# Rewrite of a gated attention and linear-attention kernel: row-tiled scores, column-tiled P.V, exponentials shared between ScalarE and VectorE, instruction order from a list scheduler

## Chip, cores, metric

One core of one Trainium2 chip. Times are device microseconds (us) of one execution; most are medians of four runs. A profiled run also has a span (first to last instruction, about 1.9 us less than its time) and a mean granted TensorE clock, where 1.0 is full speed.

## The reference

Two attention blocks read the same x (2048 x 512, 32 heads of 16) and are mixed by a gate. Block A is softmax attention, block B linear attention. Shortened:

```python
g = sigmoid((x * gate_w).sum(-1, keepdims=True))
# A: per head, Dh = 16
p = softmax(einsum("bhqd,bhkd->bhqk", q, k) * Dh ** -0.5)
a = einsum("bhqk,bhkd->bhqd", p, v)  ... @ A_wo
# B: phi(t) = where(t > 0, t + 1, exp(t)) + 1e-6
b = phi(q) @ (phi(k)^T v) / (phi(q) @ sum(phi(k)))  ... @ B_wo
return g * a + (1 - g) * b
```

Block A costs 32 heads x 2048 x 2048 exponentials: 2048 blocks of 128 keys x 512 queries. That decides the time.

## The kernel before

The kernel works in 32 rounds of four heads and 512 queries, 64 blocks each. K is copied four times with all but one head's 16 rows set to zero, so that a score matmul can read all 128 rows of the array. Three blocks at a time land in three banks of PSUM (the memory that matmuls write to; the kernel lays it out as eight banks of 512 columns), ScalarE exponentiates all three in one instruction, and P.V takes P as the weights and V (with a column of ones for the denominator) as the moving operand. VectorE has the projections' copies, the K masks and block B.

```python
# scores: full array, K zero-padded to one head
f_mm(RINGB[b0 + k], KTpad[:, hs, j, 128 * kb:128 * (kb + 1)], QT[:, par, qc, :], start=True, stop=True)
# exponentials: three banks, 128x1536, in one instruction
nc.scalar.activation(PT[:, slot, 0:512 * n], ps[:, 512 * b0:512 * (b0 + n)], ACT.Exp, scale=SCALE)
# P.V: 12 small matmuls a group, 128 x 32 out
f_mm(acc[:, 128 * qbl + 32 * j:128 * qbl + 32 * (j + 1)],
     PT[:, slot, 512 * k + 128 * qbl:512 * k + 128 * (qbl + 1)], Vaug[:, hs, kb, j, :], start=first, stop=False, sg=True)
# ... (projections, block B, gate and output are cut)
```

The softmax here doesn't subtract the row's maximum and nothing guards it: scores larger than these inputs give would overflow.

## Time and profile before

| | before |
|---|---|
| time, median (range) | 972.5 us (972.0 to 973.2) |
| ScalarE busy | 945.0 us, 97% of the span |
| TensorE busy, mean granted clock | 832.4 us, 0.993 |
| VectorE busy | 305.9 us, 32% |

ScalarE is the bound: 934.2 us of exponentials with 10.6 us idle before them, most of that before the first one. TensorE waits for ScalarE, not the other way round.

One stretch of the steady part, from the view of windows. The columns are the busy us of TensorE, weight loads, VectorE, ScalarE and GpSimd, then the granted clock, DMA share and GB/s.

```profile
300.00:500.00 200.00, 173.42 (x2316) 104.56 (x2358) 65.64 (x139) 199.80 (x160) 0.00 (x0) 1.00 0.01 2
```

### The profile page before, as it was taken

How to read it: one execution, taken by the hardware profiler on the slowest of the kernel's cores; microseconds unless marked ns; L12 is line 12 of the kernel's file. 1: busy time of each engine (PE TensorE's matmuls, PEld its weight loads, DVE VectorE, ACT ScalarE, POOL GpSimd, SP SyncE). 2: the span in 40 equal slices, each digit the busy share in tenths (PEclk: the TensorE clock that was granted, in tenths of full speed). 3: DMA queues.
4: the chain of work that ended last, by engine and by line, in shares of the span. 5: the costliest groups of instructions: out<-in, count | busy, mean ns of one | idle time of the engine just before them, and what ended most of it. 6: DMA issues, size and time to landing. Idle time of an engine off the chain costs nothing.

```text
span 970.5 us, 25037 instructions
## 1 busy us (share of the span) xinstructions
PE 832.4 (86%) x11257; PEld 504.8 (52%) x11464; DVE 305.9 (32%) x591; ACT 945.0 (97%) x739; POOL 8.1 (1%) x42
## 2 busy tenths in 40 slices
PE   6988888898888988888888888888888898879886
PEld 3555555555555555555545555554555555545553
DVE  3311132032321223223654445344555431102112
ACT  3999999999999999999999999999999999999996
POOL 3000000000000000000000000000000000000000
PEclk8999999999999999999999999999999999999998
DMA  9000000000000000000000000000000000000001
GB/s 275 3 2 1 2 2 1 2 1 2 2 2 2 2 1 2 1 2 2 2 1 2 2 1 2 2 1 1 1 2 2 1 2 1 1 2 18 12 18 45
DMA packets 13067, 10.40 MB, mean 11 GB/s; under 512 B 6816, under 2 KB 11936, under 8 KB 12960
## 3 DMA queue, kind: packets, MB, share of 16 engines
q1 hardware_dynamic: 8768, 7.34, 2.5%
q10 hardware_dynamic: 4192, 1.44, 0.7%
q8 instruction: 90, 1.47, 0.6%
q14 instruction: 17, 0.14, 0.1%
HBM read 5.64 MB, written 2.10 MB: 8 GB/s over the span
## 4 chain that ended last, share of the span: by engine, by line
ACT 52%; PE 30%; issue 14%; DVE 2%; DMA 1%; ACTq 1%; DVEq 0%
ACT PT L730 51%; PE ps L307 30%; DVE den L613 1%; ACT epool L514 1%; DMA wA_5<-in_A_wqkv_dram 1%; DVE tpool L516 1%; ACTq L273 0%; DVE outt L677 0%; DVE den L607 0%; PE ps L310 0%; DMA out_dram<-outt 0%; DVE KTpad L425 0%; ACTq L992 0%; ACTq L985 0%; DVE KT L413 0%
## 5 line engine op out<-in xcount | busy, mean ns | idle before, releaser
L730 ACT ACTIVATE PT<-ps 128x1536 bf16<-128x1536 f32 (+1 forms) x704 | 934.2, 1465 | 10.6 <-PE ps L307 9.5
L307 PE MATMUL ps<-QT,KTpad 128*128 128x512 bf16 x1883 | 529.4, 381 | 116.6 <-ACT PT L730 108.4
L307 PEld LDWEIGHTS ps<-Vaug,PT 128*128 128x128 bf16 x8192 | 308.0, 96 | 166.7 <-ACT PT L730 0.8
L307 PE MATMUL ps<-Vaug,PT 128*128 128x32 bf16 x8192 | 313.8, 176 | 1.0 <-ACT PT L730 0.4
L307 PEld LDWEIGHTS ps<-QT,KTpad 128*128 128x128 bf16 x2048 | 152.4, 97 | 247.6 <-ACT PT L730 139.9
L756 DVE RECIPROCAL rden<-ps 128x16 f32<-128x16 f32 x32 | 8.2, 257 | 190.8 <-PE ps L307 190.8
L613 DVE RECIPROCAL den<-den 128x128 f32<-128x128 f32 x64 | 61.0, 953 | 2.2
L516 DVE COPY tpool<-ps 128x512 f32<-128x512 f32 x32 | 22.1, 691 | 91.0 <-ACT epool L514 91.0
L465 DVE CAST Vaug<-ps 128x256 bf16<-128x256 f32 x32 | 13.6, 424 | 78.9 <-PE ps L307 78.9
L425 DVE TENSOR_SCALAR KTpad<-KT,maskK 128x512 bf16<-128x512 bf16 x128 | 34.6, 346 | 0.1
L307 PE MATMUL ps<-wB,xT 128*128 128x512 bf16 x116 | 31.1, 377 | 3.1 <-DVE tpool L516 2.6
L564 DVE TENSOR_TENSOR kvacc<-ps,kvacc 128x258 f32<-128x258 f32 x32 | 13.7, 428 | 57.4 <-PE ps L307 57.4
L307 PE MATMUL ps<-xT,wA 128*128 128x512 bf16 x100 | 27.0, 377 | 0.5
L482 DVE CAST QT<-ps 128x512 bf16<-128x512 f32 x16 | 11.1, 691 | 42.4 <-PE ps L307 42.4
L413 DVE CAST KT<-ps 128x512 bf16<-128x512 f32 x16 | 11.1, 692 | 39.4 <-PE ps L307 39.4
L514 ACT ACTIVATE epool<-ps 128x512 f32<-128x512 f32 x32 | 21.8, 682 | 0.0
L677 DVE SCALAR_TENSOR_TENSOR outt<-ps,gom,bB 128x512 bf16<-128x512 f32 x16 | 11.8, 749 | 28.3 <-PE ps L307 26.8
L645 DVE TENSOR_SCALAR bB<-ps,gom 128x512 bf16<-128x512 f32 x16 | 12.0, 750 | 26.6 <-PE ps L307 26.6
L607 DVE TENSOR_SCALAR den<-ps 128x512 f32<-128x512 f32 x16 | 11.1, 691 | 29.6 <-PE ps L307 29.6
L307 PE MATMUL ps<-wA,xT 128*128 128x64 bf16 x448 | 18.7, 192 | 0.0
L307 PE MATMUL ps<-woA,OT 128*128 128x512 bf16 x58 | 16.6, 390 | 0.8 <-DVE OT L667 0.6
L667 DVE COPY OT<-ps 128x512 bf16<-128x512 bf16 (+2 forms) x20 | 7.1, 369 | 30.9 <-PE ps L310 30.9
(61 smaller groups left out, 246.1 us busy)
## 6 DMA issues: line engine op xcount, KB each, us to landing
out_dram<-outt SPq DMA_DIRECT2D x16, 128.0 KB, 1.7
wA<-in_A_wqkv_dram SPq DMA_DIRECT2D x1, 1536.0 KB, 7.0
wB<-in_B_wqkv_dram SPq DMA_DIRECT2D x1, 1536.0 KB, 10.3
xnat<-in_A_x_dram ACTq DMA_DIRECT2D x2, 512.0 KB, 5.3
woA<-in_A_wo_dram SPq DMA_DIRECT2D x1, 512.0 KB, 11.3
woB<-in_B_wo_dram SPq DMA_DIRECT2D x1, 512.0 KB, 12.2
wA_5<-in_A_wqkv_dram ACTq DMA_DIRECT2D x3, 128.0 KB, 6.9
xT<-in_A_x_dram SPq DMA_TRANSPOSE x8, 6.0
```

Of the source, the lines that this page charges most:

```text
L307: return lambda: nc.tensor.matmul(o, lhsT=l, rhs=r, start=start, stop=stop, skip_group_check=sg)
L413: op(DV, lambda par=par, t=t, sp_=sp_: nc.vector.tensor_copy(KT[:, par, 512 * t:512 * (t + 1)], sp_), reads=[rsp], writes=[r_KT[par][t]])
L425: op(DV, lambda hs=hs, j=j, t=t, par=par, half=half: nc.vector.tensor_scalar(KTpad[:, hs, j, 512 * t:512 * (t + 1)], KT[:, par, 512 * t:51 ...
L465: op(DV, lambda hs=hs, vb=vb, nb=nb, src=src: nc.vector.tensor_copy(Vaug[:, hs, vb:vb + nb, :, 0:16], src), reads=[rsp], writes=[r_Vaug[hs ...
L482: op(DV, lambda par=par, qc=qc, sp_=sp_: nc.vector.tensor_copy(QT[:, par, qc, :], sp_), reads=[rsp], writes=[r_QT[par][qc]])
L514: ev_e = op(AC, lambda e_s=e_s, sp_=sp_: nc.scalar.activation(epool[:, e_s, :], sp_, ACT.Exp), reads=[rsp], writes=[r_e[e_s]])
L516: op(DV, lambda e_s=e_s, sp_=sp_: nc.vector.tensor_copy(tpool[:, e_s, :], sp_), reads=[rsp], writes=[r_t[e_s]], extra=[ev_e])
L564: op(DV, lambda srcv=srcv, dstv=dstv: nc.vector.tensor_tensor(dstv, srcv, dstv, ALU.add), reads=[rsp, r_kvacc], writes=[r_kvacc])
L613: op(DV, lambda s=s, c4=c4: nc.vector.reciprocal(den[:, s, 128 * c4:128 * (c4 + 1)], den[:, s, 128 * c4:128 * (c4 + 1)]), reads=[r_den[s]] ...
L645: op(DV, lambda qc=qc, qbl=qbl, qb=qb, sp_=sp_: nc.vector.tensor_scalar(bB[:, qc, qbl, :], sp_, gom[:, 1, qb:qb + 1], None, op0=ALU.mult), ...
L677: op(DV, lambda s3=s3, qb=qb, qc=qc, qbl=qbl, sp_=sp_: nc.vector.scalar_tensor_tensor(out=outt[:, s3, :], in0=sp_, scalar=gom[:, 0, qb:qb ...
L730: op(AC, lambda slot=slot, b0=b0, n=n: nc.scalar.activation(PT[:, slot, 0:512 * n], ps[:, 512 * b0:512 * (b0 + n)], ACT.Exp, scale=SCALE), ...
```

## The change

The intent is to take exponentials off ScalarE. VectorE gets about a fifth of the key blocks and computes 2^t as the mean of four shifted piecewise-linear terms: the score plus a constant, written as int16, is the bit pattern of a bf16 near 2^t, and three more terms are that integer plus 26, 56 and 94. All four are multiplied with V as if they were four P blocks, so such a block costs four P.V waves (a wave is up to four tiled matmuls that run at the same time; in the trace one P.V wave starts 0.22 us after another at full clock) instead of one. To make room on TensorE, scores read only their 32 rows (four heads at once) and P.V makes V the weights, 17 columns in one of four column tiles, four heads at once. A list scheduler at build time picks the order and gives each key block to ScalarE or VectorE. Core of the diff, much cut:

```diff
-                fns.append(f_mm(RINGB[b0 + k], KTpad[:, hs, j, 128 * kb:128 * (kb + 1)], QT[:, par, qc, :],
-                                start=True, stop=True))
+            return mm(bank(b), KT[32 * j:32 * (j + 1), t8 % 2, 128 * kb:128 * (kb + 1)],
+                      Qz[32 * j:32 * (j + 1), qslot(r), par, :])
 ... (cut)
+            return C(DV, 400, 692, lambda: nc.vector.tensor_scalar(
+                Z[:, z, 512 * j:512 * (j + 1)], bank(5), ZB, 0.0, op0=ALU.add, op1=ALU.max),
 ... (cut)
+            return C(DV, 300, 690, lambda: nc.vector.tensor_scalar(Z[:, z, :], Z[:, z0, :], float(m), None, op0=ALU.add),
 ... (cut)
+            return C(AC, 500, 427 * n + 63, lambda: nc.scalar.activation(
+                P[:, slot, 0:512 * n], bank(b0, n), ACT.Exp, scale=ESC),
 ... (cut)
+            for j in range(4):
+                fns.append(mm(ps[32 * j:32 * j + 17, 3584:4096], Vc[:, t8 % 2, w["kb"], 2 * j + par, 0:17], w["aps"][j],
+                              start=first, stop=False, sg=True))
 ... (cut: the scheduler's choice of the next instruction)
+                if c.E is PE and c.mode and c.mode != st["mode"]:
+                    a = max(a, PE.free + 40.0)
```

PSUM is split into a set of three banks and one of two for ScalarE, one bank for VectorE's scores, one for everything else and one accumulator.

## The prediction

> **What bounds the kernel now.** ScalarE. The profile's busy table gives it 945.0 of 970.5 us (97%); the windows show it busy 199.3 to 199.8 us in each 200 us from 100 to 900. Nearly all is one group, the softmax exponentials: 704 activations, 934.2 us. From 16.6 to 961 us ScalarE works through 32 rounds of 20 three-bank and 2 two-bank exponentials and one 512-wide one; solved with one fixed cost per instruction beside 1280, 853 and 427 ns of streaming, that is 77 ns: 1.357, 0.930 and 0.504 us (estimates). TensorE is 86% busy but waits 109 us for ScalarE, VectorE is 32% busy, GpSimd 1%. Head 16.6 us, tail after the last exponential about 8.5 us.
>
> **What the change does** (counts from the instruction order).
> - ScalarE: exponentials fall from 640 three-bank + 64 two-bank (2048 score blocks) to 323 + 323 + one single (1616 blocks). 432 blocks, 21%, go to VectorE. ScalarE: 323 x (1.357 + 0.930) + 33 x 0.504 + about 4 = 760 us, 185 us less.
> - VectorE: 432 conversions out of PSUM at 0.691 us (the trace's duration for 128x512 fp32 from PSUM) = 299 us; 324 adds over 128x2048 int16. [...] I estimate 0.69 us each = 224 us; about 190 other operations, 130 us. Sum 650 us, up from 306.
> - TensorE: 8192 narrow P.V matmuls become 3344 in 836 column-tiled waves of four (1728 of them, 432 waves, for spline terms); the scores are row-tiled by four without the masked K copies. At 0.216 us for each concurrent wave (512 columns; estimate): scores about 800 x 0.216 = 173, P.V 181, rest 138: 490 us, plus about 1490 switches between tilings. [...] no trace here shows its cost yet. [...]
> - GpSimd: about 130 real operations, [...]
>
> **How much lies on the critical path.** ScalarE stays the bound, so its 185 us are nearly all worth time, but it will no longer be 99.9% fed: its two score buffers are three and two banks, [...] TensorE's fixed order also waits for VectorE. I allow 5 to 8% idle in ScalarE's steady stretch, 40 to 60 us. Head about 11 us (K and Q weights first, first block of x by small loads), tail about 9 us. 11 + 760 + 45 + 9 = 825 us. Range 790 to 870.
>
> Chances: faster by over 2% 0.95, within 2% 0.03, slower 0.02.
>
> **What would show it.** ScalarE 755 to 770 us busy, 90 to 95% of the span, idle before exponentials put down to score matmuls; VectorE 640 to 690 us, int16 adds 0.69 us undisturbed; score and P.V groups of four ending within about 0.25 us beyond one matmul's latency; first exponential at 10 to 13 us.
>
> **What would make it wrong.** Tiled matmuls that don't run concurrently (then TensorE alone needs over 1100 us); [...] tiling switches above 0.2 us, making TensorE the bound at 850 us or more; or a schedule matching the chip better than I allow, about 790 us.

The forecast's sum is whole: 11 + 760 + 45 + 9 = 825 us. In the trace of the kernel before, 128x512 matmuls start 0.216 us after one another (median), and activations that follow one another without a wait start 1.330 us apart over three banks and 0.477 us over one; over two it is 0.904 us in the changed kernel's trace, so about 0.427 us a bank.

## More of the kernel before

From the profile page of the kernel before: busy time of each engine, the busy tenths of ScalarE and the granted TensorE clock in 40 slices of the span, and the costliest group (busy us, mean ns of one, then idle time before them).

```profile
span 970.5 us, 25037 instructions
...
PE 832.4 (86%) x11257; PEld 504.8 (52%) x11464; DVE 305.9 (32%) x591; ACT 945.0 (97%) x739; POOL 8.1 (1%) x42
...
ACT  3999999999999999999999999999999999999996
...
PEclk8999999999999999999999999999999999999998
...
L730 ACT ACTIVATE PT<-ps 128x1536 bf16<-128x1536 f32 (+1 forms) x704 | 934.2, 1465 | 10.6 <-PE ps L307 9.5
L307 PE MATMUL ps<-QT,KTpad 128*128 128x512 bf16 x1883 | 529.4, 381 | 116.6 <-ACT PT L730 108.4
```

The clock row, which is easily passed over, is at 9 (90% or more) in all but the first and last slice.

## The result

| | before | after |
|---|---|---|
| time, median | 972.5 us | 880.1 us (872.9 to 888.3) |
| ratio to before, 95% interval | | 0.9025 (0.899 to 0.906) |
| ScalarE busy | 945.0 us | 770.9 us, 89% |
| TensorE busy | 832.4 us | 789.5 us, 91% |
| mean granted clock, profiled run | 0.993 | 0.855 |

A ratio here is always the mean time of one kernel's fast runs over that of the other's fast runs of the same rounds, so it isn't quite the ratio of the medians. One of the four runs (888.3 us, clock 0.834) counts as slow, being over 1.5% above the fastest, and is left out of the ratio. Clock and time go together within the four: 0.834 and 0.855 are the ends of one, 888.3 and 872.9 us of the other.

The change is clearly faster, but it misses the forecast of 825 us and its range of 790 to 870. The same page lines as before, of the changed kernel, with the chain of work that ended last by engine (the line that begins with PE 65%):

```profile
span 871.0 us, 15840 instructions
...
PE 789.5 (91%) x6283; PEld 210.7 (24%) x6345; DVE 625.0 (72%) x978; ACT 770.9 (89%) x686; POOL 145.4 (17%) x155
...
ACT  5999999877999988999798999978879779899984
...
PEclk7999999865999979999597999968759569699966
...
PE 65%; ACT 15%; DVE 11%; issue 9%; DMA 0%; POOL 0%; ACTq 0%; SPq 0%; POOLq 0%
...
L631 ACT ACTIVATE P<-ps 128x1536 bf16<-128x1536 f32 (+1 forms) x647 | 753.5, 1263 | 75.9 <-PE ps L323 73.0
L576 DVE TENSOR_SCALAR Z<-ps 128x512 int16<-128x512 f32 x432 | 295.6, 684 | 182.4 <-PE ps L323 180.4
L598 DVE TENSOR_SCALAR Z<-Z 128x2048 int16<-128x2048 int16 x324 | 228.0, 731 | 3.4
```

Put the ACT and PEclk rows under each other: ScalarE's dips lie where the clock is low. The busy work came out as planned (770.9 us on ScalarE, 625.0 on VectorE). What is new is 75.9 us of idle time before exponentials, 73.0 of it put down to TensorE, and TensorE's 65% of the chain that ended last.

The view of windows of the changed kernel, for a stretch at half clock and the next at full clock:

```profile
620.00:650.00 30.00, 28.95 (x169) 5.34 (x162) 17.20 (x26) 21.39 (x19) 4.03 (x4) 0.50 0.05 10
652.00:674.00 22.00, 18.67 (x186) 5.26 (x182) 18.98 (x32) 22.00 (x20) 1.24 (x3) 1.00 0.05 13
```

At half clock TensorE is busy 28.95 of 30 us and ScalarE only 21.39. At full clock ScalarE is busy all 22.00. Over the whole steady part I cut the trace at every change of the clock and summed such windows: ScalarE is busy 75.1% of 206 us at half clock and 96.9% of 577 us at full clock. The recorded clock is only ever 1.0 or 0.5 (44 stretches), in stretches that are multiples of 3.41 us (the last, cut off by the end, aside); a mean of 0.855 is 29% of the span, 253 us, at half speed.

What half clock does to one wave (here of 512 columns) is in the timeline of TensorE's matmuls (start us, us, then what). First a stretch at half clock:

```profile
632.23 1.03 PE L323 MATMUL ps<-Z,Vc 128*17 128x512 bf16 x8
633.20 0.60 PE L323 MATMUL ps<-Qz,KT 32*128 32x512 bf16 x2
633.74 0.61 PE L323 MATMUL ps<-P,Vc 128*17 128x512 bf16 x4
634.27 1.03 PE L323 MATMUL ps<-Qz,KT 32*128 32x512 bf16 x4
```

Then one at full clock:

```profile
656.59 0.39 PE L323 MATMUL ps<-Qz,KT 32*128 32x512 bf16 x2
656.91 0.39 PE L323 MATMUL ps<-P,Vc 128*17 128x512 bf16 x4
657.13 0.39 PE L323 MATMUL ps<-Z,Vc 128*17 128x512 bf16 x4
...
658.25 0.40 PE L323 MATMUL ps<-P,Vc 128*17 128x512 bf16 x4
658.48 0.39 PE L323 MATMUL ps<-Z,Vc 128*17 128x512 bf16 x4
```

Read starts, not durations. At full clock one P.V wave follows another after 0.22 us (656.91 to 657.13), so the four tiles do run together; a P.V wave follows a score wave after 0.32 us (656.59 to 656.91), so a switch of tiling costs about 0.10 us. At half clock two waves take 0.42 us longer than one (1.03 against 0.61; the x8 and the last x4 are two waves each, the x4 three scores and then one), and wave plus switch take 0.54 us.

### The profile page after: what moved, and what is told of

Its sections match the earlier page's. It is cut to its first block, busy times and chain, and to the rows that moved or that the text cites. A ratio compares the mean times of both kernels' runs of the same rounds, so it can differ in the third digit from the quotient of the medians.

```text
span 871.0 us, 15840 instructions
## 1 busy us (share of the span) xinstructions
PE 789.5 (91%) x6283; PEld 210.7 (24%) x6345; DVE 625.0 (72%) x978; ACT 770.9 (89%) x686; POOL 145.4 (17%) x155
## 4 chain that ended last, share of the span: by engine, by line
PE 65%; ACT 15%; DVE 11%; issue 9%; DMA 0%; POOL 0%; ACTq 0%; SPq 0%; POOLq 0%
PE ps L323 65%; ACT P L631 14%; DVE Z L576 6%; DVE Z L598 2%; DVE T L829 1%; DVE mb L854 0%; ACT eb L853 0%; DVE outt L975 0%; DVE Vc L797 0%; DMA out_dram<-outt 0%; DVE KT L752 0%; DVE QT L774 0%; DVE rec L836 0%; PE ps L728 0%; DVE dn L926 0%
## 5 line engine op out<-in xcount | busy, mean ns | idle before, releaser
L631 ACT ACTIVATE P<-ps 128x1536 bf16<-128x1536 f32 (+1 forms) x647 | 753.5, 1263 | 75.9 <-PE ps L323 73.0
L576 DVE TENSOR_SCALAR Z<-ps 128x512 int16<-128x512 f32 x432 | 295.6, 684 | 182.4 <-PE ps L323 180.4
L323 PE MATMUL ps<-Qz,KT 32*128 32x512 bf16 x2048 | 373.7, 432 | 48.0 <-ACT P L631 25.9
L598 DVE TENSOR_SCALAR Z<-Z 128x2048 int16<-128x2048 int16 x324 | 228.0, 731 | 3.4
L323 PE MATMUL ps<-Z,Vc 128*17 128x512 bf16 x1728 | 183.5, 441 | 13.7 <-DVE Z L598 5.0
L323 PE MATMUL ps<-P,Vc 128*17 128x512 bf16 x1616 | 177.4, 432 | 1.0 <-DVE T L829 0.8
L323 PEld LDWEIGHTS ps<-Qz,KT 32*128 32x128 bf16 x2048 | 82.4, 93 | 336.2 <-ACT P L631 130.8
L856 POOL TENSOR_SCALAR eb<-eb 128x512 f32<-128x512 f32 x32 | 66.0, 2064 | 213.8 <-DVE mb L854 194.7
L323 PEld LDWEIGHTS ps<-Z,Vc 128*17 128x17 bf16 x1728 | 40.6, 90 | 97.4 <-issue 31.5
L857 POOL TENSOR_TENSOR phiK<-eb,mb 128x512 bf16<-128x512 f32 x32 | 43.7, 1367 | 2.7
## 6 DMA issues: line engine op xcount, KB each, us to landing
xnat<-in_A_x_dram SPq DMA_DIRECT2D x3, 512.0 KB, 12.7
```

The costliest lines, as they stand in the source:

```text
L323: return lambda: nc.tensor.matmul(o, lhsT=l, rhs=r, start=start, stop=stop, skip_group_check=sg)
L576: return C(DV, 400, 692, lambda: nc.vector.tensor_scalar(Z[:, z, 512 * j:512 * (j + 1)], bank(5), ZB, 0.0, op0=ALU.add, op1=ALU.max), [r_b ...
L598: return C(DV, 300, 690, lambda: nc.vector.tensor_scalar(Z[:, z, :], Z[:, z0, :], float(m), None, op0=ALU.add), [r_Z[z0]], [r_Z[z]], after ...
L631: return C(AC, 500, 427 * n + 63, lambda: nc.scalar.activation(P[:, slot, 0:512 * n], bank(b0, n), ACT.Exp, scale=ESC), [r_bank[b0 + k] fo ...
L856: yield po(800, lambda: nc.gpsimd.tensor_scalar(eb[:, i, :], eb[:, i, :], 1.0, 1e-6, op0=ALU.min, op1=ALU.add), [r_eb[i]], [r_eb[i]])
L857: yield po(1300, lambda: nc.gpsimd.tensor_tensor(dst_ap, eb[:, i, :], mb[:, i, :], ALU.add), [r_eb[i], r_mb[i]], dst_res)
```

## The experiments

The question is why ScalarE starves. Three theories. **Clock**: tiled matmuls leave TensorE so little active that its clock is halved in stretches (29% of the span above), and TensorE can't feed ScalarE then (busy 75.1%). **Switches**: 1490 changes of tiling, 0.1 us each, are what TensorE has too much of. **Order**: the fixed order fits the chip badly, and a low clock only follows from the waiting. All results below were correct, and each had its runs of the kernel before (972.2 to 972.3 us). Time and clock are of all four runs, medians for the time.

| run | time us | granted clock | ratio to before |
|---|---|---|---|
| after | 880.1 | 0.834 to 0.855 | 0.9025 |
| f_full | 823.5 | 0.981 to 0.996 | 0.8471 |
| f_col | 813.5 | 0.987 to 0.996 | 0.8373 |
| f_col1 | 813.6 | 0.987 to 0.994 | 0.8369 |
| f_half | 841.9 | 0.911 to 0.928 | 0.8654 |
| f_row1 | 879.9 | 0.863 to 0.941 | see text |
| b_row1 | 1474.2 | 0.504 to 0.516 | 1.5165 |
| b_row4 | 988.4 | 0.687 to 0.704 | 1.0166 |
| p_sw | 859.0 | 0.861 to 0.877 | 0.8805 |
| p_fill | 807.7 | 0.979 to 0.993 | 0.8312 |
| p_fill1 | 812.6 | 0.974 to 0.991 | 0.8377 |
| n_dve (two runs) | 1002.4 | 0.987 to 0.990 | 1.031 |

### f_full: the changed kernel plus useless full-array matmuls

```diff
             if c.E is PE and c.mode:
+                rr_ = st["pv_round"]
+                if rr_ < NR and st["acc_free"] and not st["first"][rr_] and st["waves_left"][rr_] > 0:
+                    for _ in range(int((start - PE.free) // 216.0)):
+                        PE.add(mm(bank(7), warm[:, 0:128], xT[:, 0, 0:512], start=False, stop=False, sg=True), [r_warm.w], inc=False)
                 st["mode"] = c.mode
```

The weights are zeros and the sum goes into the P.V accumulator while only TensorE uses it, so nothing changes in the result, and the order of everything else stays.

> The changed kernel in the same order, plus 385 full-array matmuls of 128x512 with zero weights, added into the P.V accumulator (so they add nothing) where the plan leaves TensorE idle for at least 0.216 us before its next instruction: about 83 us more TensorE work, the result unchanged. Theory clock (the granted TensorE clock falls to half when TensorE is too little active, and ScalarE starves in those stretches): the mean granted clock rises from 0.855 to 0.93 or more, and the kernel gets faster although it does more, 835 to 865 us. Theory switches (tiling switches and TensorE's own work bound it): 83 us more work and some 300 more switches make it slower, 890 us or more, whatever the clock. Theory order (the planned order fits the chip badly, the clock only follows from it): time within 1% of 880 or slower, ScalarE's idle time as large at full clock.

Measured: 823.5 us at clock 0.99. The kernel does more on TensorE and is 57 us faster (880.1 - 823.5). Switches and order both wanted the opposite.

### f_col: the same with column-tiled fillers

```diff
-                        PE.add(mm(bank(7), warm[:, 0:128], xT[:, 0, 0:512], ...
+                        for j_ in range(4):
+                            PE.add(mm(ps[32 * j_:32 * j_ + 17, 3584:4096], warm[:, 0:17], xT[:, 0, 0:512], start=False, stop=False, sg=True), [r_warm.w], inc=False)
```

> As the run with full-array fillers, in the same 385 places, but each filler is a column-tiled wave of four 17-column matmuls with zero weights. Theory clock, if activity is counted as time in which a matmul streams: clock and time as with full-array fillers, within 1%. Theory clock, if activity is counted by the share of the array in use: less clock than with full-array fillers. Theory switches: a little faster than the full-array fillers, since fewer switches are added, but slower than 880 us.

Measured: 813.5 us, clock 0.987 to 0.996: the same clock as with f_full, and 10 us faster, just over the 1% allowed. That fits the switches which f_full adds (the traces, which lack some filler records, hold 1767 in f_full and 1662 in f_col: 105 more, at 0.10 us each); no run isolates it. Page lines of this run, then the same two windows as above:

```profile
PE 773.9 (95%) x7817; PEld 229.4 (28%) x7885; DVE 621.9 (77%) x978; ACT 766.1 (94%) x686; POOL 145.9 (18%) x155
...
ACT  5999999999999999999999999999999999999995
...
PEclk7999999999999999999999999999999999999999
...
L631 ACT ACTIVATE P<-ps 128x1536 bf16<-128x1536 f32 (+1 forms) x647 | 749.2, 1259 | 27.7 <-PE ps L323 24.4
```

```profile
620.00:650.00 30.00, 29.63 (x325) 8.31 (x321) 25.07 (x41) 29.94 (x28) 1.25 (x3) 1.00 0.07 15
652.00:674.00 22.00, 21.14 (x184) 5.60 (x186) 16.93 (x29) 21.37 (x19) 0.84 (x2) 1.00 0.08 19
```

The clock row is full, ScalarE's dips are gone, and its idle time before exponentials fell from 75.9 to 27.7 us while its work stayed (753.5 and 749.2 us).

### f_row1 and f_col1: what counts as activity

In the same 385 places, a filler that streams the same 512 columns but uses a quarter of the array's rows, or a quarter of its columns:

```diff
+ f_row1:               PE.add(mm(bank(7), warm[0:32, 0:128], xT[0:32, 0, 0:512], start=False, stop=False, sg=True), [r_warm.w], inc=False)
+ f_col1:               PE.add(mm(ps[0:17, 3584:4096], warm[:, 0:17], xT[:, 0, 0:512], start=False, stop=False, sg=True), [r_warm.w], inc=False)
```

> Control for the fillers: the same 385 places of the same order, and each filler streams the same 512 columns, but it is one 32-row tile (32 x 128 zero weights), a quarter of the array's rows. Theory clock, activity counted by the share of the array: it takes TensorE's time and adds little activity, so the clock stays below 0.92 and the time at 870 us or more, unlike the 813 and 823 us of the two fillers that fill the array. Theory place (the fillers help by holding TensorE in those gaps, not by activity): 810 to 830 us as the other fillers.

> As the run before, but each filler is one column tile with all 128 rows and 17 columns, a quarter of the array's columns. If activity counts rows alone, clock 0.97 or more and 810 to 825 us; if it counts the area of the array in use, clock below 0.92 and 865 us or more.

Measured: f_col1 813.6 us at clock 0.99, as good as four tiles. f_row1 874.1, 885.8, 885.8 and 836.1 us at clocks 0.879, 0.863, 0.863 and 0.941. The last run counts as fast, the other three as slow, so no ratio is given. Even that one is 20 us above the slowest run of f_col1 (816.0), though it beats the runs without fillers; for this one run the expectation (870 or more, clock below 0.92) failed, for the other three it held. Fast runs alone give the same order, but f_row1 has only this one. So a filler of 32 rows helps unreliably, one of 128 rows and 17 columns helps fully, although it covers fewer cells of the array (128 x 17 = 2176 against 32 x 128 = 4096): rows in use count, the area in use doesn't explain it, 17 columns are enough here, and holding TensorE in the gap is not what helps. The ScalarE and clock rows of the profiled run of f_row1 (one of the slow three) still dip together; f_col1's don't:

```profile
ACT  5999999986679899999879899989967899999895
...
PEclk8999999975559799999778899979955699999799
```

```profile
ACT  5999999999999999999999999999999999999995
...
PEclk7999999999999999999999999999999999999999
```

### f_half: the dose

```diff
-                    for _ in range(int((start - PE.free) // 216.0)):
+                    for _ in range(1 if (start - PE.free) >= 432.0 else 0):
```

> Dose: full column-tiled filler waves (four tiles) only in the 103 gaps that the plan leaves at 0.432 us or more, 22 us of filling instead of 83. Theory clock: between the kernel without fillers (clock 0.85, 880 us) and with 385 (0.99, 813 us): clock 0.90 to 0.97, 825 to 860 us.

Measured: 841.9 us, clock 0.911 to 0.928. Between the two, as expected: 103 filler waves buy 38 us, 385 buy 67.

### b_row1 and b_row4: row tiles alone, in the kernel before

Both give the kernel before 32-row score matmuls and change nothing else but the pairing of heads with rows that this needs (the changes to V's columns, masks and output columns are cut here).

```diff
-                fns.append(f_mm(RINGB[b0 + k], KTpad[:, hs, j, 128 * kb:128 * (kb + 1)], QT[:, par, qc, :],
+                fns.append(f_mm(RINGB[b0 + k], KTpad[32 * j:32 * (j + 1), hs, j, 128 * kb:128 * (kb + 1)], QT[32 * j:32 * (j + 1), par, qc, :],
```

In b_row4 the blocks of a group also come from different row groups, so that they run together:

```diff
-            return [(u % NTB, u // NTB) for u in range(start, start + sizes[gi])]
+            return [(u // 4, u % 4) for u in range(start, start + sizes[gi])]
```

> The kernel before with one thing changed: each score matmul reads only the 32 rows that hold its head (the heads of a round are paired to rows so that this works), three of the same rows after one another, so that none run at the same time. TensorE's streaming time is unchanged (2048 x 0.216 us). Theory clock, activity as streaming time: clock 0.98 to 0.99 as before, time within 1% of 972 us. Theory clock, activity as the share of the array in use: the clock falls below 0.9 and the time rises to 985 us or more. Theories switches and order: row tiles alternate with full-array P.V twice per group, some 1400 switches; if these cost 0.1 us each, TensorE has 140 us more to do in 970 and the time rises by a few per cent at full clock.

> As the run before it, but the units of a group are taken from different 32-row groups, so that three score matmuls run at the same time: 704 waves x 0.216 = 152 us of streaming where the kernel before has 442, everything else alike. Theory clock (streaming time counts): TensorE's activity falls to some 62%, the clock falls to half in stretches (mean 0.75 to 0.92), and the kernel is not faster or is even slower than 972 us (975 to 1030), though TensorE has 290 us less to do. Theory switches: slower than 972 us at full clock. Theory order: 965 to 975 us at clock 0.98 or more, ScalarE still bound.

Measured: b_row1 1474 us at clock 0.51, b_row4 988 us at clock 0.70 (a little below the range given). The page of b_row1, then of b_row4:

```profile
PE 1442.9 (98%) x11380; PEld 517.1 (35%) x11464; DVE 307.0 (21%) x591; ACT 1009.9 (68%) x739; POOL 8.1 (1%) x42
...
PEclk6555555555555555565555555555555555555555
```

```profile
PE 810.8 (82%) x11380; PEld 400.7 (41%) x11464; DVE 306.2 (31%) x591; ACT 943.4 (96%) x739; POOL 8.1 (1%) x42
...
PEclk9857777677666877777656676767685776756567
```

b_row1 is the cleanest case of all. TensorE is busy 98% of the span and its clock stays at half nearly throughout, so its clock did not follow the time that it is busy. b_row4 streams its scores in a third of the waves (704 against 2048 matmuls), is busy less (82%), has as many switches (1408 in either trace), and yet gets more clock (0.70): it has up to 96 rows in use where b_row1 has 32. And with 290 us less score streaming by estimate than the kernel before, it is 1.7% slower than it (interval 1.5 to 1.8%, so beyond the noise): ScalarE gets 96% instead of 97%.

### p_sw, p_fill, p_fill1: a plan that knows what a switch costs

```diff
-                    a = max(a, PE.free + 40.0)
+                    a = max(a, PE.free + 100.0)
```

This gives 1038 switches instead of 1491 and 112 key blocks on VectorE instead of 108. p_sw has no fillers, p_fill the 383 column-tiled filler waves that this plan has room for, p_fill1 466 single-tile fillers, also in gaps from 0.15 us.

> The scheduler told that a tiling switch costs 0.10 us, as in the run with 112 blocks on VectorE, but no fillers at all: 1038 switches instead of 1491. Theory switches or order: the better fitting plan helps by itself, 780 to 850 us. Theory clock: the rows of the array that matmuls use per microsecond stay about the same, the clock stays at half for a good part (mean 0.80 to 0.90), and the time is 860 to 890 us, like the changed kernel.

> Search for a better version: as the 385 column-tiled fillers, but the scheduler is told that a switch of tiling costs TensorE 0.10 us (the timeline shows about that) and not 0.04. Its plan then has 1038 switches instead of 1491, and 112 key blocks on VectorE instead of 108. If switches matter on the chip, 450 fewer of 0.1 us take 45 us from TensorE, and as TensorE is now 95% busy in the 813 us run, the time falls to 785 to 805 us; if TensorE isn't what holds ScalarE up there, 808 to 818 us.

> That plan with single-column-tile fillers (one matmul instead of four, since rows alone seem to count), and a filler already in gaps of 0.15 us: 466 instead of 383. Theory clock: clock steadily 0.99 and 800 to 808 us; if the longer filling delays score matmuls, 808 to 820 us at that clock.

Measured: p_sw 859.0 us at clock 0.87: outside both ranges, 1 us below that of theory clock and 9 above that of switches or order. The better plan is worth 2.4% (0.8805 / 0.9025) without fillers, a third of what the fillers bring; its clock is also a little higher and ScalarE has 16 of its 1616 score blocks fewer, so this isn't the switches alone. p_fill 807.7 us, above the 785 to 805 hoped for and at the edge of the 808 to 818 named for a TensorE that doesn't hold ScalarE up: 450 fewer switches bring 6 us beside f_col, not 45, and ScalarE's exponentials alone are 11 us shorter (737.9 against 749.2), so switches don't hold ScalarE up much once the clock is there. p_fill1 812.6 us at a slightly lower clock, above 800 to 808 and inside the 808 to 820 expected if the longer filling delays score matmuls; whether it does was not looked at. More filling didn't help. p_fill is the best kernel: ratio 0.8312 (0.828 to 0.834) to the kernel before.

### n_dve: the change without VectorE's share

```diff
         def d_pick():
+            return
```

With the single-tile fillers of f_col1, where they fit (1644).

> The change without its VectorE share: all 2048 score blocks go to ScalarE (410 three-bank and 409 two-bank exponentials), the tiled TensorE work stays, and single-tile fillers hold the clock. ScalarE then needs about 410 x 1.357 + 409 x 0.930 + 20 = 957 us; with head, tail and 3% idle 990 to 1010 us, slower than the kernel before, which reads three banks more often. If the tiled TensorE work were where the gain comes from, it would stay below 900 us.

Measured: 1002.4 us at clock 0.99. The groups of this run:

```profile
L632 ACT ACTIVATE P<-ps 128x1536 bf16<-128x1536 f32 (+1 forms) x819 | 945.6, 1266 | 17.0 <-PE ps L323 14.5
```

With all the exponentials on ScalarE the tiled kernel is 3% slower than the old one. The run was expected at 990 to 1010 us. All of the change's gain is the fifth of the exponentials on VectorE; that the tiling is needed to make room for it is argued, since no run has VectorE's share without the tiling.

## Why the prediction was wrong

**Bound and moved work: right.** ScalarE stayed the engine that decides. Its busy time was put at 755 to 770 us and measured 770.9. VectorE was put at 640 to 690 and measured 625.0, a little below. A conversion out of PSUM was put at 0.691 us (median 0.691). An int16 add over 2048 columns was the author's estimate of 0.69 us, which the trace of the kernel before does not show (as many bf16 columns took 1.14 us there in four mask multiplies); its median is 0.686. The first exponential came at 10.5 us (10 to 13). Tiled matmuls run together at 0.22 us a wave, and a switch costs 0.10 us. n_dve shows that ScalarE's relief is the gain. Two forecasts here missed: ScalarE is busy 89% of the span, not 90 to 95%, and TensorE 789.5 us, part of it at half clock, where the forecast's 490 us with 1490 switches at the 0.10 us of the trace make 639. The two TensorE figures aren't quite the same thing: a lone wave counts 0.39 us as busy where the forecast put 0.216.

**The step that failed** is the term 45 in "11 + 760 + 45 + 9", the "5 to 8% idle in ScalarE's steady stretch, 40 to 60 us". That was made with "0.216 us for each concurrent wave", a full-clock figure, for the whole span. The prediction doesn't mention the clock; the kernel before ran at 0.993. In the profiled run, ScalarE's first and last exponentials span 10.5 to 858.3 us, 847.8 us, with 766.7 us busy (770.9 less 4.2 at the two ends): 81 us idle, not 45. The tail is 12.7 us instead of 9, itself at half clock in part. So 10.5 + 766.7 + 81 + 12.7 = 871 us; that run's time is 1.9 us more than its span, and the median run, at a lower clock, is 7 us more. Of the idle time, 51 us lie in the 206 us at half clock (206 x 0.249) and 18 in the 577 us at full clock (577 x 0.031); the rest lies at the edges that this cut leaves out.

**What the runs showed in its place.** In these runs the granted clock follows how many of the array's rows the matmuls use over time (0.51 with b_row1's 32-row scores, 0.86 to 0.94 with f_row1's 32-row fillers, 0.99 with f_col1's 128-row ones), and the change took that down: scores on 32 rows each in groups of one to four, and less streaming altogether. b_row1 shows this without anything else of the change but the switches, which it shares with b_row4, and f_full, f_col and f_col1 show that giving activity back gives the time back (823.5, 813.5 and 813.6 us at 0.99, from 880.1). Long waits are not what goes with the low clock: TensorE waits at most 1.6 us at a time in the changed kernel, and is busy 98% of b_row1's span. At full clock the forecast looks too careful: f_col, with the same plan and an estimated 83 us more work on TensorE, takes 813.5 us, and idles 28 us between its first and last exponential instead of 81. I had listed tiled matmuls that don't run together, slow int16 adds, dear switches and a better schedule as what could go wrong. The clock was in the profile I read and not on that list.

**GpSimd: seen in the trace, not tested.** The int16 adds' mean is 731 ns and their median 686, with a longest of 1770: 324 x 0.045 = 15 us. All 32 adds longer than 750 ns run at the same time as a GpSimd operation, and only 35 of the 292 shorter ones do; the 257 adds beside none take at most 0.696 us. So the slow adds go with GpSimd's operations, but no run isolates this, and why is not shown. GpSimd itself took 145.4 us.

**How many rows are enough** can be read from the kept traces. Cut all 13 at the clock's own grid of 3.41 us and add up, for each stretch, rows times columns streamed (a wave of column tiles counted once), in units of one 128-row matmul of 512 columns; a stretch at full clock has room for about 16 at 0.216 us each. Of 2421 full-clock stretches after which the clock stayed, 2350 had 6.4 units or more (median 9.5); of 114 after which it fell to half, 108 had less (median 5.0). Taken in pairs, one of each kind, the stretch after which the clock stayed has more rows in 99% of pairs, but more of the array's area only in 93% and more busy time of TensorE in 95%. So about 40% of the rows, over one stretch, was enough here. This is a correlation in traces that lack a few matmul records, but b_row1 and f_col1 point the same way by experiment.

**Left open.** Between f_half (clock 0.92) and f_col (0.99) lies the needed dose of fillers for this plan. Whether the value of the operands matters was not tried: the fillers' weights are zeros, and they sufficed.

## What to carry to other kernels

Tiling matmuls to a quarter of the rows, so that several run at once, takes fewer waves (b_row4 needs 704 for 2048 score matmuls), but when TensorE then uses fewer of its rows, its clock can be at half for part of the time (mean 0.70 there, 0.855 in the changed kernel), and an engine that it feeds starves although TensorE had time to spare at full clock (ScalarE was busy 75.1% at half clock, 96.9% at full). Look at the granted clock by slices first, next to the busy row of the engine that bounds the kernel, and for a forecast ask whether the change lowers the rows in use, not only whether TensorE has room. Where it does, matmuls with zero weights over all 128 rows and few columns, put into gaps that the plan leaves on TensorE, are cheap: here they turned 880 into 814 us, at clock 0.99 (f_col1).
